# A head-normalised attention kernel: q and k prepared apart at the start, the order planned on exact times, the last stores behind the branch

## The chip, the cores and the metric

The kernel runs on one core of a Trainium2 chip. The metric is the device time of one execution in microseconds (us). Before the change it is 594.08 us, the median of three runs (593.81 to 594.42). A core has five engines that work at the same time and meet through semaphores: TensorE (PE, matrix products; its weight loads are shown as PEld), VectorE (DVE), ScalarE (ACT), GpSimd (POOL) and SyncE (SP), which mostly issues DMA transfers. Each engine takes its instructions strictly in the order of its own queue.

## The reference

There are 32 heads of 2048 rows with 20 elements each, in bf16. Rows of q and k are divided by their length, so logits are cosines times a factor t per head; then softmax and the product with v:

```python
qn = q / (jnp.sqrt((q * q).sum(axis=-1, keepdims=True)) + eps)
kn = k / (jnp.sqrt((k * k).sum(axis=-1, keepdims=True)) + eps)
logits = jnp.einsum('bhqd,bhkd->bhqk', qn, kn) * t[None, :, None, None]
attn = _softmax(logits, axis=-1)
return jnp.einsum('bhqk,bhkd->bhqd', attn, v)
```

## The kernel before, in words

**Tiles.** Four heads form a group; there are eight groups, and in each four blocks of 512 q columns. Group and block together are a "superblock" (32 in all). In a superblock each head has 16 "units": 128 rows of k against 512 columns of q. A unit's logits come from one matmul (`qk_mm`, seen at L793) into PSUM, its exponentials are taken, and they are multiplied with v by one or more matmuls (`pv_mm`, L815) that accumulate in one PSUM bank per superblock. There are 32*64 = 2048 units. A column of ones beside v gives the softmax's sum.

**Two ways to take an exponential.** Most units go in "waves" of two to ACT (L995), through `psA` into `pA`. The others are taken by DVE: one instruction "P1" (L361) turns logits in `psD` into the bits of a 16-bit float in `dI`, and two shifted copies `dS` (mostly on POOL, L374) correct it; such a unit needs four matmuls with v where an ACT unit needs one. One of the four uses `vhalf`, half of v. This way is used only if t is not too large. So the program has a branch: DVE takes the largest t into `tmx` (L578, the "flag"), each engine loads it at its own place in its queue (L1432) and branches (L1433) into the plan with both ways or the one with ACT alone.

**Preparation.** q and k are loaded with 16 rows per partition; rows 0 to 3 of the first group come first. DVE squares (L291), sums (L294); ACT takes the square root (L309); DVE adds eps (L310), takes the reciprocal (L322), multiplies q's by t (L344) and scales k and q into `kpad` and `qpad` (L338). In the first group rows 0 to 3 are turned by matmuls with an identity (L624) and copied to `kT` and `qT` (L636 on ACT, L639 on DVE); rows 4 to 7 of k likewise a little later (L658, L664); rows 8 to 15 of k and 4 to 15 of q by a DMA transpose issued by SP (L446). Later groups go through DMA transposes wholly and are prepared while the group before is computed. Before the first turning PE multiplies zeros, 18 matmuls of 512 columns (L616, `HEAT0`), and small ones (L612) later where it would stand idle. The identity itself is built on DVE out of counters (L559 to L568).

**The order.** Nothing is scheduled on the chip. When the program is built, `make_plan` simulates all engines on a clock of 0.005 us steps with cost constants (`dve`, `ACT0`, `TS`, `LOAD0` and others), decides at each step what each engine takes next by readiness and priorities, and writes each engine's instructions down in that order; semaphore waits follow from the dependencies. DVE's way starts when the share of issued units in the first group passes `D_FROM`. `ORDER` is a string: for every ten waves one character picks a variation of the rules from `CHOICES`. In this simulation an instruction begins on a step of the clock, after the engine is free.

**The end.** After the last matmul DVE transposes the sums out of PSUM (L386), takes reciprocals (L400) and multiplies (L401); two stores, one issued by SP and one by ACT (L458), write the last part. SP first waits for all older stores (L1416). Both stores are the last instructions inside the branch; then SP waits for the two (L1439), and all engines meet at the end of the function (L173).

Of the kernel before, what the change touches and what calls it, by code (L numbers as in the profile page):

```python
# [33 lines left out]
ORDER = "01i6e8h7238em08g57h5hi2i0gi1j2i0lgea8aa50a567i6538abh965h237050"  # L34

PARTS = ((0, 4), (4, 16))
NH = 4
# [7 lines left out]
D_FROM = 0.12  # L45
# [14 lines left out]
DT = 0.005  # L60
END_MIN = 1
TS = .213
PACK = 0
JOINT = -9
HEAT0 = 18
# [6 lines left out]
ACT0 = .0633  # L72
# [84 lines left out]
def bass_standalone__qk_norm__prompt_kernel(  # L157
# [15 lines left out]
    with ExitStack() as es:  # L173
# [45 lines left out]
        out_sems = {}  # L219

# [27 lines left out]
        def prep_ops(hg, r0, r1, a0=0, a1=2, pool=False):  # L248
# [106 lines left out]
            return ops  # L355

# [112 lines left out]
        def make_plan(share):  # L469
# [42 lines left out]

            def want_dve(op, prio):
# [44 lines left out]
            for ap_, x, key in zs:  # L558
                want_dve(Op("DVE", "z", lambda e, ap_=ap_, x=x: e.memset(ap_, x), ["idn"] * (key[0] == "idb"), [key], 0.07, 0.3), 0)  # L559
            n0 = [("num", a) for a in range(8)]  # L560
            for b in (1, 2, 3):
                want_dve(Op("DVE", "z", lambda e, b=b: e.tensor_single_scalar(n4[:, :, b:b + 1], n4[:, :, 0:1], float(b), ALU.add),
                            n0, [("num", -b)], 0.08, 0.4), 0)
            nums = n0 + [("num", -b) for b in (1, 2, 3)]
            want_dve(Op("DVE", "z", lambda e: e.transpose(numT, num), nums, ["numT"], 0.15, 0.4), 0)
            want_dve(Op("DVE", "z", lambda e: e.tensor_tensor(numE, num, numT, ALU.is_equal), nums + ["numT"], ["numE"], 0.15, 0.4), 1.6)
            i4, e4 = idn[:, :].rearrange("p (a b) -> p a b", b=32), bass.AP(accT, numE.offset, [numE.ap[0], [0, 4], [1, 32]])
            want_dve(Op("DVE", "z", lambda e: e.tensor_tensor(i4, i4, e4, ALU.mult), ["idn", "numE"] + [("idb", a) for a in range(4)], ["idn", ("accT", 0)], 0.25, 0.4), 1.6)  # L568
# [6 lines left out]
            def t_load():  # L575
# [4 lines left out]
                want_dve(dve("z", H, R1, lambda e: e.tensor_copy(tb2[:, :, 0, :], tb16[:, :].rearrange("p (g h) -> p g h", h=NH)), ["tb1", "tb"], ["tb2"]), 1.45)  # L580
# [13 lines left out]
            for o in prep_ops(0, 0, 4, 0, 2):  # L594
                if o.name == "nrm":
                    o.eng = "ACT"
                    act_ops.append(P.link(o))
                    a = Op("ACT", "tab", lambda e: e.activation(act_scr[:, 16:32], act_scr[:, 16:32], ACT.Exp),
# [23 lines left out]
            psQ = psD[:, QW:2 * QW]  # L622
            for w_, pad, T, bank, key in (("k", kpad, kT, psD, ("psD", 0)), ("q", qpad, qT, psO, ("psD", OB(0)))):
                mms = [lambda e, r=r, w_=w_, pad=pad, bank=bank: e.matmul((bank if w_ == "k" or r < 2 else psQ)[:, r * 128:(r + 1) * 128],  # L624
                                                                   pad[0][:, r, :, :].rearrange("p h d -> p (h d)"), idn[:, :])
                       for r in range(4)]
                op = Op("PE", "T" + w_, None, [(w_ + "pad", 0, r) for r in range(4)] + [(w_ + "z", 0), "idn"],
                        [key] + [("psD", 1)] * (w_ == "q"))
                op.info = mms
                pe_pre.append(P.link(op))  # L630

            kk, qq = [("kT", 0, r) for r in range(4)], [("qT", 0, r) for r in range(4)]
# [16 lines left out]
            pe_mid = []  # L649
            gate = ("qT", 0, 1)  # L650
            for r0, r1, a0, a1 in ((4, 16, 1, 2), (4, 16, 0, 1)):
                for o in prep_ops(0, r0, r1, a0, a1):
                    if o.name == "sq":
                        o.reads.append(gate)
# [833 lines left out]
```

## Time and profile before

| what | value |
|---|---|
| median of three runs | 594.08 us |
| the profiled execution's own time | 594.49 us |
| its span, first to last instruction | 592.7 us |
| ACT busy / DVE busy / PE busy / POOL busy | 580.4 / 574.6 / 581.3 / 500.9 us |
| first exp begins | 9.47 us |
| first P1 begins | 23.32 us |
| last store issued | 588.52 us |
| waves on ACT, units on DVE | 628, 792 |

A line of instructions in order of time has the start, the stretch it covers, engine, line, operation, output and inputs, the count merged into it, and in brackets the engine's idle time before with what ended it. A line of groups has the busy time and the mean duration of one instruction in ns; since instructions overlap in an engine's pipeline, a mean duration is longer than the distance from one to the next. The lines of one source line's queue instructions (a letter q behind the engine) give the count, the duration in ns as least, median and most, and the first and last start. Landing is the time from a transfer's issue until its data are there.

### The profile page before, as it was taken

The numbers are of one execution on the slowest core, as the hardware profiler recorded it, in microseconds if no ns is written. First come the engines' busy times: TensorE is split into PE (matmuls) and PEld (weight loads), VectorE is DVE, ScalarE is ACT, GpSimd is POOL, SyncE is SP. The second block draws the span as 40 slices with busy tenths as digits, with TensorE's granted clock in tenths as the row PEclk, the third lists the DMA queues.
The fourth block names the chain that finished last, engine by engine and source line by source line (L and its number), as shares of the span: only waits on it lengthen the run. The fifth ranks groups of instructions, "written<-read, shape, count | busy, mean of one in ns | idle before, by whom it ended". The sixth has DMA issues, their size and how long they took to land.

```text
span 592.7 us, 16383 instructions
## 1 busy us (share of the span) xinstructions
PE 581.3 (98%) x6768; PEld 160.2 (27%) x6768; DVE 574.6 (97%) x1016; ACT 580.4 (98%) x636; POOL 500.9 (84%) x951
## 2 busy tenths in 40 slices
PE   8999999999999999999999999999999999999996
PEld 4432222322223222232223222222222232222221
DVE  7999999999999999999999999999999999999993
ACT  6999999999999999999999999999999999999995
POOL 2488899878988799887998889987999978999994
PEclk9999999999999999999999999999999999999999
DMA  8700405205051131504033005330406104010000
GB/s 116 108 2 14 104 2 45 47 8 110 3 59 32 31 86 13 79 1 101 19 22 71 1 19 100 24 69 10 92 2 76 32 2 72 2 25 4 7 11 11
DMA packets 132145, 24.20 MB, mean 41 GB/s; under 512 B 121312, under 2 KB 132064, under 8 KB 132064
## 3 DMA queue, kind: packets, MB, share of 16 engines
q1 hardware_dynamic: 131264, 22.96, 24.6%
q8 instruction: 55, 0.90, 0.6%
q14 instruction: 26, 0.21, 0.1%
q10 hardware_dynamic: 800, 0.12, 0.1%
HBM read 7.87 MB, written 2.62 MB: 18 GB/s over the span
## 4 chain that ended last, share of the span: by engine, by line
ACT 87%; PE 10%; DVE 2%; POOL 1%; issue 0%
ACT pA L995 87%; PE psD L815 4%; PE psA L793 3%; PE psA L616 1%; PE psD L612 1%; POOL dS L374 1%; DVE dI L361 0%; PE psD L793 0%; PE psD L749 0%; DVE ssum L294 0%; DVE accT L386 0%; DVE sqs L291 0%; DVE kpad L338 0%; PE psD L616 0%; DVE ost L401 0%
## 5 line engine op out<-in xcount | busy, mean ns | idle before, releaser
L995 ACT ACTIVATE pA<-psA 128x1024 f16<-128x1024 f32 (+1 forms) x628 | 576.2, 1201 | 0.5 <-PE psD L793 0.2
L374 POOL INT64_ADD dS<-dI x935 | 494.5, 545 | 71.3 <-DVE ost L401 14.3
L361 DVE TENSOR_SCALAR dI<-psD 128x512 int16<-128x512 f32 (+1 forms) x768 | 488.1, 695 | 4.3 <-PE psD L793 2.5
L793 PE MATMUL psA<-qT,kT 32*128 32x512 bf16 x1256 | 246.4, 384 | 3.7 <-ACT pA L995 1.0
L793 PE MATMUL psD<-qT,kT 32*128 32x512 bf16 x795 | 237.6, 383 | 0.1
L815 PE MATMUL psD<-dS,vaug 128*22 128x512 f16 x1584 | 201.2, 383 | 0.1
L815 PE MATMUL psD<-pA,vaug 128*22 128x512 f16 (+1 forms) x1256 | 181.1, 383 | 0.3 <-POOL dS L374 0.3
L815 PE MATMUL psD<-dI,vaug 128*22 128x512 f16 x792 | 133.9, 383 | 0.0
L815 PE MATMUL psD<-dI,vhalf 128*22 128x512 f16 x792 | 131.4, 383 | 0.0
L793 PEld LDWEIGHTS psA<-qT,kT 32*128 32x128 bf16 x1256 | 59.0, 90 | 241.1 <-ACT pA L995 235.5
L793 PEld LDWEIGHTS psD<-qT,kT 32*128 32x128 bf16 x795 | 57.3, 91 | 11.1 <-DVE dI L361 4.8
L815 PEld LDWEIGHTS psD<-dS,vaug 128*22 128x22 bf16 x1584 | 42.9, 89 | 58.2 <-issue 38.2
L815 PEld LDWEIGHTS psD<-pA,vaug 128*22 128x22 bf16 x1256 | 39.6, 89 | 49.6 <-issue 41.2
L815 PEld LDWEIGHTS psD<-dI,vhalf 128*22 128x22 bf16 x792 | 29.7, 89 | 27.4 <-issue 20.0
L815 PEld LDWEIGHTS psD<-dI,vaug 128*22 128x22 bf16 x792 | 30.3, 89 | 23.4 <-issue 16.7
L386 DVE STREAM_TRANSPOSE accT<-psD 128x512 f32<-128x512 f32 x32 | 22.6, 705 | 4.6 <-PE psD L815 4.6
L401 DVE TENSOR_TENSOR ost<-accT,rec 128x320 bf16<-128x320 f32 x32 | 17.0, 532 | 0.1
L264 DVE TENSOR_TENSOR sqs<-qk 128x1280 bf16<-128x1280 bf16 x14 | 11.7, 835 | 0.0
L749 PE MATMUL psD<-ind,sqT 128*128 128x128 bf16 x140 | 11.3, 220 | 0.0
L612 PE MATMUL psD<-zt 128*128 128x128 bf16 x123 | 10.3, 221 | 0.0
L749 PEld LDWEIGHTS psD<-ind,sqT 128*128 128x128 bf16 x140 | 7.9, 98 | 4.5 <-issue 3.6
L612 PEld LDWEIGHTS psD<-zt 128*128 128x128 bf16 x123 | 7.0, 98 | 4.9 <-issue 4.9
(59 smaller groups left out, 84.7 us busy)
## 6 DMA issues: line engine op xcount, KB each, us to landing
vaug<-in_v_dram SPq DMA_DIRECT2D x32, 80.0 KB, 4.3
qk<-in_k_dram SPq DMA_DIRECT2D x7, 320.0 KB, 4.0
out_dram<-ost SPq DMA_DIRECT2D x28, 80.0 KB, 1.9
qk<-in_q_dram SPq DMA_DIRECT2D x6, 320.0 KB, 4.3
qk<-in_q_dram SPq DMA_DIRECT2D x4, 80.0 KB, 3.0
out_dram<-ost SPq DMA_DIRECT2D x7, 40.0 KB, 2.1
qk<-in_k_dram SPq DMA_DIRECT2D x1, 240.0 KB, 3.7
qk<-in_q_dram SPq DMA_DIRECT2D x1, 240.0 KB, 4.3
```

What stands on the lines that cost most here:

```text
L264: ops.append(dve("sq", w_, R2, lambda e, o=sq, x=x3: e.tensor_tensor(o, x, x, ALU.mult), [("qk", b, a, i) for i in parts] + [("qkx", b, i) ...
L361: lambda e: e.tensor_scalar(dst, psD[:, pb * QW:(pb + n) * QW], 1024.0 * LOG2E, 15360.0 - 1024.0 * LOG2K + SHIFTS[0], ALU.mult, ALU.add),
L374: lambda e: e.int64_add(o.bitcast(U64), x.bitcast(U64), add), rd, wr)
L386: return dve("drain", QW, R1, lambda e: e.transpose(accT[:, 16 * b:16 * b + 16, :].rearrange("p b d -> p (b d)"), psO_(sb)), [("psD", OB(s ...
L401: dve("omul", 320 * n, R1, lambda e: e.tensor_tensor(dst, num, rcb, ALU.mult), at + ar, [("ost", hg % 2, g) for g in range(g0, g1)]),
L612: return lambda e: e.matmul(bank, zt[:, 0:128], zt[:, 0:n], start=False, stop=False, skip_group_check=True)
L616: o.info = [lambda e: e.matmul(psO[:, :], zt[:, 0:128], zt[:, :])] + [(lambda e, i=i: e.matmul(psA[:, (i % 3) * QW:(i % 3 + 1) * QW], zt[: ...
L749: mms = [lambda e, g=g, j=j: e.matmul(dst, sqT[:, (5 * g + j) * 128:(5 * g + j + 1) * 128], ind[:, j, 96 - 32 * g:224 - 32 * g], start=g + ...
L793: return lambda e: e.matmul(dst, lhsT, rhs, tile_position=(32 * hh, 0))
L815: return lambda e: e.matmul(dst, lhsT, rhs, start=first, stop=last, skip_group_check=True, tile_position=(0, 32 * hh))
L995: a = Op("ACT", "exp", lambda e, s=src, d=dst: e.activation(d, s, ACT.Exp), [("psA", slot)], [("pA", pslot, i) for i in range(WAVES[slot]) ...
```

## The change

The diff has four parts.

1. Rows 0 to 3 of the first group are prepared by a new function `first_ops`: q and k each have their own square, sum, square root, eps and reciprocal, written down with q ahead; k's scaling is cut into rows 0 and 1, and rows 2 and 3. The turnings follow: q first, then k's rows 0 and 1, then k's rows 2 and 3 into another bank, with 3, 3 and 6 small zero products around them (`WARM`). The copies are q's by DVE and ACT, k's first two rows by ACT, its next two by DVE. `HEAT0` goes from 18 to 11. The identity's last steps get the first priority. The later preparation of q no longer waits for rows 4 to 7 of `kT`.
2. DVE's way of taking exponentials starts earlier (`D_FROM` from 0.12 to 0.07).
3. The simulation lets an ACT or DVE instruction begin at the exact time within a step at which engine and inputs are free (`exact`); a DVE instruction costs 0.065 instead of 0.069 beside its elements, ACT's constant is 0.0634 instead of 0.0633, and there is a new `ORDER`.
4. The last two stores stand behind the branch and wait for a semaphore of their own (`fin_sem`), which the last multiplication sets. SP's waits for the older stores also move behind the branch.

```diff
-ORDER = "01i6e8h7238em08g57h5hi2i0gi1j2i0lgea8aa50a567i6538abh965h237050"
+ORDER = "42711eji12k7d5l79657bj0ldifi7fc7g9jcbm72glei3ma9gglljgm190dig74"
-D_FROM = 0.12
+D_FROM = 0.07
-HEAT0 = 18
+HEAT0 = 11
+WARM = (3, 3, 6)
+CPQ = ("DVE", "ACT")
-ACT0 = .0633
+ACT0 = .0634
...
-            o = Op("DVE", name, emit, reads, writes, cost=0.069 + c + ncols_fix,
+            o = Op("DVE", name, emit, reads, writes, cost=0.065 + c + ncols_fix,
...
+        def first_ops():
+            sqf, redf, nrmf, epsf, invf, scf = [], [], [], [], [], []
+            T_ = lambda tl, a: tl[:, a, :, 0:4]
+            for a, pad, nm in ((0, qpad, "qpad"), (1, kpad, "kpad")):
...
+                for c0, c1 in ((0, 4),) if a == 0 else ((0, 2), (2, 4)):
...
+            n_sq[0] = 0
+            return sqf + redf + nrmf + [epsf[0]] + invf[0:2] + [scf[0], epsf[1], invf[2]] + scf[1:]
...
+            def exact(eng, op, other=0.0):
+                st = max(free_[eng], ready_at(op) or 0.0, other)
+                return st if now - DT < st <= now else now
...
-            for o in prep_ops(0, 0, 4, 0, 2):
+            for o in first_ops():
...
+            pe_pre.extend([warm(WARM[0]), turn("q", 0, 4, [psO, psO, psQ, psQ], [("psD", OB(0)), ("psD", 1)]), warm(WARM[1]),
+                           turn("k", 0, 2, [psD] * 2, [("psD", 0)]), warm(WARM[2])])
+            pe_mid = [turn("k", 2, 4, [psK] * 2, [("psD", 2)])]
...
-            copy("ACT", kT, psD, 0, 128, [("psD", 0)], kk[:1])
-            copy("DVE", qT, psO, 0, 256, [("psD", OB(0))], qq[:2])
-            copy("ACT", qT, psQ, 256, 512, [("psD", 1)], qq[2:])
-            copy("ACT", kT, psD, 128, 512, [("psD", 0)], kk[1:])
+            copy(CPQ[0], qT, psO, 0, 256, [("psD", OB(0))], qq[:2])
+            copy(CPQ[1], qT, psQ, 256, 512, [("psD", 1)], qq[2:])
+            copy("ACT", kT, psD, 0, 256, [("psD", 0)], kk[:2])
+            copy("DVE", kT, psK, 256, 512, [("psD", 2)], kk[2:])
...
-                finish(a, now, a.cost, a.lat)
-                free_["ACT"] = now + a.cost
+                st = exact("ACT", a)
+                finish(a, st, a.cost, a.lat)
+                free_["ACT"] = st + a.cost
...
+                st = exact("DVE", o, lock[0] if o.port else 0.0)
+                finish(o, st, o.cost, o.lat)
+                free_["DVE"] = st + o.cost
...
+                if o.name == "out" and o.sem in ends:
+                    assert o is P.order[e][-1] and [d.sem for d in o.deps] == [fin_sem]
+                    continue
...
+            if e == "SP":
+                for x in plans[0][0].order["SP"]:
+                    if x.name == "out" and x.sem not in ends:
+                        eng.wait_ge(x.sem, 16)
+            for o in plans[0][0].order[e][-1:]:
+                if o.name == "out":
+                    eng.wait_ge(fin_sem, 1)
+                    o.emit(eng).then_inc(o.sem, 16)
```

More of the change, by code (lines that the diff above doesn't have):

```diff
@@ L219, in bass_standalone__qk_norm__prompt_kernel @@
         out_sems = {}
+        fin_sem = sem("s_fin")
         def dma_sem():
@@ L910, in step_heat @@
                 nonlocal pe_mode, pe_t
-                if in_use() >= S.HEAT or cur == NSB or not cur_free():
+                if not waves or in_use() >= S.HEAT or cur == NSB or not cur_free():
                     return False
@@ L1220, in step_dve @@
                             return True
-                finish(o, now, o.cost, o.lat)
-                free_["DVE"] = now + o.cost
+                st = exact("DVE", o, lock[0] if o.port else 0.0)
+                finish(o, st, o.cost, o.lat)
+                free_["DVE"] = st + o.cost
                 return True
@@ L1410, in issue @@
             P, waits = plan
-            outs = [o for o in P.order["SP"] + P.order["ACT"] if o.name == "out"]
             for o in P.order[e][i0:i1]:
-                if e == "SP" and o.name == "out" and o.sem is ends[0]:
-                    for x in outs:
-                        if x.sem not in ends:
-                            eng.wait_ge(x.sem, 16)
+                if o.name == "out" and o.sem in ends:
+                    assert o is P.order[e][-1] and [d.sem for d in o.deps] == [fin_sem]
+                    continue
                 for s_, val in waits[id(o)]:
```

78 lines of the change are left out of this document (49 added, 29 removed).

## The prediction, made before the changed kernel ran

> **What bounds the kernel now.** I read the page's busy times and groups first, then the instructions in order of time at both ends, then the chain.
>
> ```profile
> PE 581.3 (98%) x6768; PEld 160.2 (27%) x6768; DVE 574.6 (97%) x1016; ACT 580.4 (98%) x636; POOL 500.9 (84%) x951
> ...
> L995 ACT ACTIVATE pA<-psA 128x1024 f16<-128x1024 f32 (+1 forms) x628 | 576.2, 1201 | 0.5 <-PE psD L793 0.2
> L361 DVE TENSOR_SCALAR dI<-psD 128x512 int16<-128x512 f32 (+1 forms) x768 | 488.1, 695 | 4.3 <-PE psD L793 2.5
> ```
> ```profile
> 51.27 517.24 ACT pA L995 x564
> ```
>
> Two engines share the exponentials. ACT takes 628 waves of two units (1256), DVE the other 792 of 2048 units (768 instructions, 24 of them double). The chain's middle is 564 exps in 517.24 us: 0.917 each. An instruction's own duration includes its pipeline, so a pitch is a stretch less one duration (1.20 for an exp by its group, 0.68 for a single P1 by shape), over the count less one:
>
> ```profile
> 195.23 19.35 ACT L995 ACTIVATE pA<-psA 128x1024 f16<-128x1024 f32 x21
> ```
> ```profile
> L361 DVE TENSOR_SCALAR dI<-psD 128x512 int16<-128x512 f32 x744 | 460.8, 679 | 3.2 <-PE psD L793 1.4
> ```
> ```profile
> 361.09 7.80 DVE L361 TENSOR_SCALAR dI<-psD 128x512 int16<-128x512 f32 x13
> ```
> ```profile
> 361.09 3.01 DVE L361 TENSOR_SCALAR dI<-psD 128x512 int16<-128x512 f32 x5
> ```
> ```profile
> 561.14 11.65 DVE L361 TENSOR_SCALAR dI<-psD 128x512 int16<-128x512 f32 x19
> ```
>
> A good stretch of exps has (19.35-1.20)/20 = 0.907. In a good stretch of P1, eight more add 7.80-3.01 = 4.79, or 0.599; an ordinary one gives (11.65-0.68)/18 = 0.609. So neither engine has a long idle time, and both wait a little for PE's written-out order. Time can come from the start, the end, the split of units, and those small waits.
>
> **The start.** DVE, ACT and PE up to the first exp:
>
> ```profile
> 1.65 6.38 PE L616 MATMUL psA<-zt 128*128 128x512 bf16 x17
> ...
> 3.68 0.49 DVE L291 TENSOR_TENSOR sqs<-qk 128x640 bf16<-128x640 bf16 x1 [0.62 <-DMA qk<-in_q_dram]
> ...
> 4.09 0.28 DVE L568 TENSOR_TENSOR idn<-idn,accT 128x128 bf16<-128x128 bf16 x1
> ...
> 4.29 0.81 DVE L294 TENSOR_REDUCE ssum<-sqs 128x32 f32<-128x640 bf16 x1
> ...
> 5.02 0.18 DVE L578 TENSOR_REDUCE tmx<-tb 128x1 f32<-128x32 bf16 x1
> ...
> 5.14 0.23 ACT L309 ACTIVATE nr<-ssum 128x32 f32<-128x32 f32 x1 [2.29 <-DVE ssum L294]
> 5.39 1.28 ACT L598 ACT_TABLE_LOAD   x1
> 5.40 0.18 DVE L310 TENSOR_SCALAR rsa<-nr 128x32 f32<-128x32 f32 x1
> ...
> 5.62 0.35 DVE L322 RECIPROCAL rn<-rsa 128x32 f32<-128x32 f32 x1
> ...
> 6.34 0.15 PEld L616 LDWEIGHTS psA<-zt 128*128 128x128 bf16 x1 [0.28 <-issue]
> 6.41 0.17 DVE L344 TENSOR_TENSOR rn<-rn,tb 128x16 f32<-128x16 f32 x1
> 6.61 0.49 DVE L338 TENSOR_TENSOR qpad<-qk,rn 128x320 bf16<-128x320 bf16 x1
> ...
> 6.77 0.76 PEld L616 LDWEIGHTS psA<-zt 128*128 128x128 bf16 x4 [0.28 <-issue]
> ...
> 8.51 0.42 DVE L639 CAST qT<-psD 128x256 bf16<-128x256 f32 x1 [1.41 <-PE psD L624]
> 8.79 0.48 ACT L636 ACTIVATE kT<-psD 128x384 bf16<-128x384 f32 x1
> 8.97 0.73 DVE L291 TENSOR_TENSOR sqs<-qk 128x640 bf16<-128x640 bf16 x2
> ...
> 9.47 4.69 ACT L995 ACTIVATE pA<-psA 128x1024 bf16<-128x1024 f32 x5 [0.19 <-PE psA L793]
> ```
>
> q is ready at 7.10 (6.61+0.49), but PE works off zeros until 8.03: they come every 0.43 up to 6.77, then every 0.21. So the zeros set the start. Eleven of them end at 1.65+10*0.43 = 5.95, and q's path takes over. On DVE an independent successor starts 0.08 before an end (3.68+0.49 to 4.09), a dependent one about 0.03 after. The identity's product (0.20 of pitch between square and sum) moves ahead of 3.68, into the 0.62 of waiting for q. Squares and sums of 320 elements, from the groups by shape:
>
> ```profile
> L294 DVE TENSOR_REDUCE ssum<-sqs 128x16 f32<-128x320 bf16 x2 | 1.0, 486 | 0.1
> ...
> L291 DVE TENSOR_TENSOR sqs<-qk 128x320 bf16<-128x320 bf16 x2 | 0.6, 318 | 0.0
> ```
>
> By these: squares 3.68 and 3.92, sums 4.16 and 4.57, the flag 4.98, eps of q 5.08 (its square root has run since 4.69), reciprocal 5.29 to 5.54, times t 5.58 to 5.75, then q's scaling 5.84 (after k's reciprocal) to 6.33. That is 0.77 earlier, though DVE has five instructions more (two squares, sums, eps and reciprocals for one, and k's scaling in two).
>
> PE's branch waits for the flag:
>
> ```profile
> L1432 PEldq TENSOR_LOAD <-tmx x1: 483/483/483, 5.2 to 5.2; - x1
> ```
> ```profile
> L1433 PEldq COMPARE_BRANCH  x2: 89/1801/3513, 6.1 to 586.0; - x2
> ```
>
> From the flag's load to the branch's end it is 0.95, under zeros now. With the flag at its old place it ends at 6.2 again, after the eleven zeros, so three small zeros end near 6.5, and the turning of q ends at 7.0 to 7.1. ACT has two square roots (0.23 each), then the table load (1.28), ready by 6.9, under cover of DVE; without that cover it would add directly. The copies of q run 7.15 to 7.57 on DVE and ACT; k's two rows are turned meanwhile, and their copy (0.38) ends near 7.9. From a last copy's end (8.93) to the first exp (9.47) it took 0.53. First exp: 8.45, **1.0 less**. Bounds: 0.3 less (PE slow throughout and every join late) to 1.3 less.
>
> One row speaks against it: PE's pitch halves only at 6.77, after 5.5 us without a gap, and now it pauses between 5.95 and 6.2. Slow to the first exp, turnings and first products cost 0.45 more, and the total is 0.45 higher. [...]
>
> **The units that DVE takes.** DVE's own start:
>
> ```profile
> 14.69 0.69 DVE L664 CAST kT<-psD 128x512 bf16<-128x512 f32 x1 [0.49 <-PE psD L658]
> ...
> 23.32 1.23 DVE L361 TENSOR_SCALAR dI<-psD 128x1024 int16<-128x1024 f32 x1 [1.10 <-PE psD L793]
> ```
>
> DVE's later preparation begins at 7.5 instead of 8.97 (1.47); q's part no longer waits for kT (0.49); with D_FROM 0.07 instead of 0.12, P1s begin at 18 issued units instead of 31, near 8.45+7*0.917 = 14.9 (the ninth wave is issued when the seventh exp is done) instead of 23.32, so the 1.10 of idleness goes; one copy more costs 0.34. The halved v, of lower priority than all this, now comes after the first P1s; their results wait for it in a ring of 28 slots, some 17 us of P1. POOL, idle until then, starts its additions earlier. Together 2.7 us, or 4.4 units at 0.609. ACT's 1.0 is 2.2 units. Over 2/0.917+1/0.609 = 3.82 units per us, 6.6 units are 1.7 us for start and split together.
>
> Behind that a wait becomes late. Rows 8 to 15 of kT come by DMA, and SP issues them behind loads that no compute holds up:
>
> ```profile
> 11.79 5.33 SPq L437 DMA_DIRECT2D vaug<-in_v_dram  x3
> 17.16 2.05 SPq L446 DMA_TRANSPOSE kT<-kpad  x1
> ```
> ```profile
> kT<-kpad SPq DMA_TRANSPOSE x1, 4.0
> ```
>
> They land at 21.2. Rows 0 to 7 are 32 units: today issued by about 23, then by about 18.8 (18 units at 14.9, then 3.6 per us). The planner books 1.4 per v load where three took 5.33, so it does not see this. PE then stands with everything behind it; ACT, with two waves in hand, idles some 1.4 (3.1 units), while DVE partly has preparation left. I take 6.6-3.1 = 3.5 units, **0.9 less** for start and split (ends: 1.7 less, and 1.9 more in the second rival).
>
> **The end.** Queue instructions of the function's closing line, and the last stores:
>
> ```profile
> 587.94 0.49 DVE L401 TENSOR_TENSOR ost<-accT,rec 128x320 bf16<-128x320 f32 x1
> 588.46 0.67 ACTq L458 DMA_DIRECT2D out_dram<-ost  x1
> ```
> ```profile
> L173 SPq DRAIN  x1: 13/13/13, 591.1 to 591.1; - x1
> L173 ACTq DRAIN  x1: 81/81/81, 592.4 to 592.4; - x1
> ```
>
> The span ends at 592.7, on ACT's drain. ACT leaves the branch only after issuing its store (589.13) and arrives 3.3 later; SP, which saw both stores land, drains at 591.1. With the stores behind the branch, ACT jumps after dispatching its last exp (584.8, the row below) and, 3.3 later (PE's own jump took 3.5, above), arrives near 588.1 to 588.3, before the product is done at 588.43: the jump lies under drain, reciprocal and product. SP's drain is then last, **1.3 less**. Bounds: 0.4 less (ACT a microsecond late, its store late too) to 1.4. SP's sixteen waits for older stores move behind the jump too, and are over long before the last product. The last exp's start:
>
> ```profile
> L995 ACT ACTIVATE pA<-psA x628: 1018/1196/1347, 9.5 to 584.8; 128x1024 f16<-128x1024 f32 x156, 128x1024 bf16<-128x1024 f32 x1
> ```
>
> **The order in between.** New constants and the ORDER string rewrite all queues. The planner no longer rounds each ACT and DVE start up to 0.005, and a DVE step costs 0.004 less: P1 0.598, as in the undisturbed stretch. The trace cannot show the new order. Best end: all exps and P1s at their undisturbed pitch, 628*0.010 = 6.3 and 792*0.010 = 7.9 less on the two, so about 7 together. Worst: DVE is given units that it cannot hold, 3 to 5 more. The chip's mean pitches lie within 2% of the undisturbed ones and PE waits remain, so I stay near zero: **0.9 less**.
>
> **Sum.** 0.9+1.3+0.9 = 3.1 of the profiled span: 592.7 to 589.6. That execution took 594.49, 0.41 above the median; from the median, 594.08-3.1 = 591.0.
>
> **Rivals.** (1) Slower: DVE becomes the bound. It is 97% busy, and from 23.3 to 582.3 hardly idle. Each P1 unit beyond 792 costs 0.609, against 2.7+1.3 gained: even at 799 units, and ten more give +2.1, 596.2. For it: the planner's DVE got cheaper by 1%, which invites more units; against it: the pitch it now assumes is the undisturbed one. 0.09. (2) The kT rows fall behind all four v loads, landing near 23 (5.33/3 = 1.8 later): ACT idles 2.9, which takes the start's 1.0 and 1.9 more; with the end's 1.3 and no gain in the middle, 594.7. For it: q's preparation now fills k's gaps on DVE, delaying kpad; against it: loads do not depend on it. 0.12. (3) The new order removes half of the small waits: 3 less, 588.0. 0.20. (4) The start does not move, PE being slow or the branch late: 591.9. Inside the forecast, which has 0.59 with it.
>
> Shares: faster (below 592.9) 0.79, same 0.12, slower 0.09; 0.2%, 1.2 us, is what a measurement can tell from nothing. The range runs from 587.6, past rival 3, to 594.3, most of the way to rival 2; rival 1 is left out.
>
> **What would show it.** First exp at 8.4 to 8.5; q's scaling done at 6.3; PE's pitch still 0.43 for all big zeros; first P1 near 15; PE and ACT idle between 18.8 and 21.2 with kT's DMA as releaser; ACT's drain no later than SP's; P1 units between 792 and 799 and exps between 624 and 628. Wrong it goes if P1 units pass 799, if ACT's mean pitch rises over 0.92, or if DVE waits for PE in the middle.

## The result, and the profile after

The changed kernel takes 599.69 us (median of four runs, 599.26 to 599.96), the kernel before beside it 593.94 (593.57 to 594.42). The ratio is 1.0096, with a 95% interval of 1.0078 to 1.0113: it became 1% slower. The prediction said 591.0 with a range up to 594.3, so it is wrong in sign and size. The profiled execution took 599.8 us, its span is 598.1 in place of 592.7. Three executions of the experiments below ran at a clearly lower granted clock than most others of their kernel (769.92 us at 0.602 with the new start alone, 599.38 and 599.63 us at 0.977 and 0.976 with one addition of POOL ahead); they count in the medians and not in the ratios.

The page of the kernel after: busy times, the clock that PE was granted in 40 slices of 15 us, and the two groups of exponentials.

```profile
PE 583.2 (98%) x6744; PEld 156.6 (26%) x6744; DVE 575.8 (96%) x1034; ACT 577.6 (97%) x632; POOL 505.0 (84%) x947
...
PEclk9759999999999999999999999999999999999999
...
L1037 ACT ACTIVATE pA<-psA 128x1024 f16<-128x1024 f32 (+1 forms) x624 | 573.6, 1212 | 11.9 <-PE psA L833 7.7
...
L393 DVE TENSOR_SCALAR dI<-psD 128x512 int16<-128x512 f32 (+1 forms) x781 | 492.7, 689 | 14.5 <-PE psD L833 12.1
```

ACT has four exps fewer (624 for 628), DVE eight units more (800 for 792). Against that ACT was idle for 11.9 us before its exps, where it was 0.5 before, and the clock is below full in the second and third slice. Everything unusual lies ahead of 50 us.

The account is easiest on ACT. The most frequent distance between the starts of two exps is 0.9035 us in both traces, so a span is the first exp's start, plus (exps - 1) times 0.9035, plus what the single distances exceed 0.9035 by in sum ("waits"), plus what follows the last exp's start ("tail"):

| | first exp | exps | waits | of these before 50 us | tail | span |
|---|---|---|---|---|---|---|
| before | 9.47 | 628 | 8.8 | 0.9 | 8.0 | 592.7 |
| after | 7.77 | 624 | 21.1 | 13.1 | 6.3 | 598.1 |
| difference in time, from unrounded values | -1.7 | -3.6 | +12.3 | +12.3 | -1.7 | +5.3 |

So three terms went the right way, by 7.0 us together, more than the 3.1 that were predicted. One term, the waits of the first 50 us, took 12.3. Beyond 50 us the waits are the same in both. ACT's exps of that stretch, in order of time:

```profile
7.77 3.77 ACT L1037 ACTIVATE pA<-psA 128x1024 bf16<-128x1024 f32 x4 [0.49 <-PE psA L833]
12.56 8.36 ACT L1037 ACTIVATE pA<-psA 128x1024 f16<-128x1024 f32 x9 [1.02 <-PE psA L833]
26.14 1.02 ACT L1037 ACTIVATE pA<-psA 128x1024 f16<-128x1024 f32 x1 [5.22 <-PE psA L833]
27.86 1.02 ACT L1037 ACTIVATE pA<-psA 128x1024 f16<-128x1024 f32 x1 [0.70 <-PE psD L833]
29.36 1.02 ACT L1037 ACTIVATE pA<-psA 128x1024 f16<-128x1024 f32 x1 [0.48 <-PE psD L833]
```

There are three places: 1.0 of idleness ahead of 12.56, 5.2 ahead of 26.14, and then an exp every 1.5 us up to 41.5. The first two come from waits of PE, in whose queue the next products for ACT stand behind these:

```profile
11.80 0.40 PE L855 MATMUL psD<-pA,vaug 128*22 128x512 bf16 x4 [0.93 <-DMA vaug<-in_v_dram]
...
19.22 0.39 PE L833 MATMUL psA<-qT,kT 32*128 32x512 bf16 x2
24.51 0.60 PE L855 MATMUL psD<-dS,vaug 128*22 128x512 f16 x2 [4.90 <-POOL dS L406]
```

At 19.6 PE reaches the first product with a shifted copy `dS`, which POOL has not made. DVE's part was ready early, its first three P1s start at 16.84, and POOL did nothing that the profile shows (DVE, POOL, and POOL's queue instructions at the line of the additions):

```profile
16.84 2.56 DVE L393 TENSOR_SCALAR dI<-psD 128x1024 int16<-128x1024 f32 x3
```
```profile
17.64 0.39 POOL L571 MEMSET vaug<- 128x64 bf16 x1
23.77 2.37 POOL L406 INT64_ADD dS<-dI  x4 [5.73 <-issue]
```
```profile
L406 POOLq MODIFY_POOL_CONFIG  x2: 11/11/11, 18.0 to 18.0; - x2
```

A configuration instruction ran at 18.0, and the first addition at 23.77, 5.7 us later; "issue" says that the engine waited for nothing that the profile shows. The kernel before has the same thing, at the same place in POOL's queue:

```profile
L374 POOLq MODIFY_POOL_CONFIG  x2: 11/11/11, 19.2 to 19.2; - x2
```
```profile
25.35 7.38 POOL L374 INT64_ADD dS<-dI  x14 [6.93 <-DVE dI L361]
```

There the addition followed 6.2 us after the configuration, and the idle time was put down to DVE's P1. With the first P1 at 23.32 hardly anything waited for it. So both traces have a delay of about 6 us (5.7 and 6.2) between the configuration and POOL's first addition, without an instruction in it; what fills it they do not show.

The third place is the clock. Windows of the kernel after: PE's, PEld's, DVE's, ACT's and POOL's busy time with counts, granted clock, share of DMA, GB/s:

```profile
20.00:25.00 5.00, 0.49 (x4) 0.13 (x4) 0.56 (x1) 0.92 (x2) 1.24 (x3) 0.69 1.07 202
25.00:30.00 5.00, 5.00 (x35) 1.02 (x31) 2.58 (x4) 2.68 (x3) 2.68 (x6) 0.50 0.22 41
30.00:40.00 10.00, 10.00 (x69) 2.54 (x66) 6.18 (x11) 6.71 (x8) 6.08 (x12) 0.50 0.01 2
40.00:50.00 10.00, 10.00 (x117) 2.87 (x115) 9.09 (x19) 9.27 (x11) 7.17 (x14) 0.88 0.01 3
```

During the idle time the granted clock fell to half, at 21.9, and it stayed there until 42.4, although PE was busy without a gap from 24.5 on. At half the clock PE is the bound, and both other engines wait for it.

The end of the kernel after, DVE, ACT's and SP's stores, and the drains of the function's end:

```profile
594.74 0.49 DVE L433 TENSOR_TENSOR ost<-accT,rec 128x320 bf16<-128x320 f32 x1
```
```profile
595.26 0.67 ACTq L490 DMA_DIRECT2D out_dram<-ost  x1
```
```profile
L175 ACTq DRAIN  x1: 582/582/582, 596.0 to 596.0; - x1
...
L175 SPq DRAIN  x1: 13/13/13, 597.8 to 597.8; - x1
```

ACT now drains right behind its store and SP comes last, as predicted; it was ACT, 3.3 us behind its store.

### The profile page after: what moved, and what is told of

The parts are those of the page before. It is cut to its first block, busy times and chain, and to the rows that moved or that the text cites. A ratio compares the mean times of both kernels' runs of the same rounds, so it can differ in the third digit from the quotient of the medians.

```text
span 598.1 us, 16346 instructions
## 1 busy us (share of the span) xinstructions
PE 583.2 (98%) x6744; PEld 156.6 (26%) x6744; DVE 575.8 (96%) x1034; ACT 577.6 (97%) x632; POOL 505.0 (84%) x947
## 4 chain that ended last, share of the span: by engine, by line
ACT 90%; PE 7%; SPq 1%; DMA 1%; issue 1%; DVE 1%; POOL 0%
ACT pA L1037 90%; PE psD L855 3%; PE psA L833 2%; SPq L469 1%; DMA vaug<-in_v_dram 1%; PE psD L651 1%; PE psD L789 0%; PE psD L833 0%; SPq L459 0%; DVE sqs L267 0%; DVE accT L418 0%; DVE dI L393 0%; POOL dS L406 0%; DVE ost L433 0%; SPq L613 0%
## 5 line engine op out<-in xcount | busy, mean ns | idle before, releaser
L1037 ACT ACTIVATE pA<-psA 128x1024 f16<-128x1024 f32 (+1 forms) x624 | 573.6, 1212 | 11.9 <-PE psA L833 7.7
L833 PE MATMUL psD<-qT,kT 32*128 32x512 bf16 x801 | 244.4, 388 | 0.0
L855 PE MATMUL psD<-dS,vaug 128*22 128x512 f16 x1600 | 203.5, 385 | 4.9 <-POOL dS L406 4.9
L855 PE MATMUL psD<-pA,vaug 128*22 128x512 f16 (+1 forms) x1248 | 178.6, 386 | 0.9 <-DMA vaug<-in_v_dram 0.9
L855 PE MATMUL psD<-dI,vaug 128*22 128x512 f16 x800 | 136.8, 385 | 0.0
L855 PEld LDWEIGHTS psD<-pA,vaug 128*22 128x22 bf16 x1248 | 38.4, 89 | 47.1 <-issue 42.4
L789 PE MATMUL psD<-ind,sqT 128*128 128x128 bf16 x140 | 12.8, 233 | 0.0
L267 DVE TENSOR_TENSOR sqs<-qk 128x1280 bf16<-128x1280 bf16 x14 | 11.8, 843 | 0.0
L432 DVE RECIPROCAL rec<-accT 128x16 f32<-128x16 f32 x32 | 7.5, 234 | 0.1
L325 DVE RECIPROCAL rn<-rsa 128x128 f32<-128x128 f32 (+1 forms) x9 | 7.4, 827 | 0.0
```

The costliest lines, as they stand in the source:

```text
L267: ops.append(dve("sq", w_, R2, lambda e, o=sq, x=x3: e.tensor_tensor(o, x, x, ALU.mult), [("qk", b, a, i) for i in parts] + [("qkx", b, i) ...
L325: add("inv", lambda e: e.reciprocal(rn_, ra), [K("ra")], RN[a0:a1], R1, n * 5 * R1)
L432: dve("rec", 16 * n, R1, lambda e: e.reciprocal(rc, aT[:, :, D]), at, ar, 16 * n * 5 * R1),
L789: mms = [lambda e, g=g, j=j: e.matmul(dst, sqT[:, (5 * g + j) * 128:(5 * g + j + 1) * 128], ind[:, j, 96 - 32 * g:224 - 32 * g], start=g + ...
L833: return lambda e: e.matmul(dst, lhsT, rhs, tile_position=(32 * hh, 0))
L855: return lambda e: e.matmul(dst, lhsT, rhs, start=first, stop=last, skip_group_check=True, tile_position=(0, 32 * hh))
```

## The experiments

Two theories stood against each other. A: the 12.3 us are POOL's invisible 5.7 us, and the clock that PE's idleness costs behind it. (The expectations call this delay the loading of the additions' code. That is the author's reading; no trace shows it.) B: the new order itself is at fault (DVE has too many units, or the parts of the change don't fit each other), and the gap would open elsewhere. All times are medians, each with its ratio to the kernel before on the same chip; readings of a trace are those of one profiled execution.

### The gap filled with zeros, so that the clock stays

The wait for POOL stays, but PE multiplies 80 zeros of 128x128 ahead of it:

```diff
+                if e == "PE" and any(s_ is sems["POOL"] and val >= first_add.get(id(P), 1e9) for s_, val in waits[id(o)]):
+                    first_add.pop(id(P))
+                    for _ in range(FILL):
+                        eng.matmul(psO[:, 0:128], zt[:, 0:128], zt[:, 0:128], start=False, stop=False, skip_group_check=True)
                 for s_, val in waits[id(o)]:
                     eng.wait_ge(s_, val)
```

> The changed kernel with 80 small zero products put into PE's queue just ahead of its first wait for a shifted copy, where it stood idle from 19.6 to 24.4; all queues are otherwise the same. If the half clock is caused by PE's idleness and costs what follows it: the wait of ACT near 20 to 26 us remains (5 us), the clock stays at full and exps from 27 us on come every 0.92 instead of 1.5: about 6 us less, 593.5. If the half clock comes from something else, the time stays at 599 to 600.

593.13 us, ratio 0.999 (0.9972 to 1.0008); nine of ten executions took 593.0 to 593.5, and one 598.12 at a granted clock of 0.988. The windows of this run have the full clock throughout:

```profile
20.00:30.00 10.00, 9.31 (x134) 5.86 (x130) 4.45 (x9) 5.00 (x7) 4.98 (x11) 1.00 0.83 123
30.00:50.00 20.00, 19.91 (x244) 5.79 (x240) 19.87 (x37) 20.00 (x24) 17.14 (x33) 1.00 0.01 2
```

The waits between 25 and 50 us fall from 6.5 to 0.25, and the long one near 20 stays (5.2 over the usual distance, 5.4 in the kernel after). So the lost clock alone is worth 6.3 us, and the gap the other 5.4. Zeros do nothing for the kernel but keep the clock.

### The same zeros behind the gap

The same loop with `FILL = 48` stands behind the wait for POOL: the clock falls, and PE then gets products over the full 128 rows and columns.

> The changed kernel with 48 small zero products on the whole array put just behind PE's first wait for a shifted copy (near 24.4), where the clock is already halved and PE then works without a break for 18 us at half speed. If the clock returns when the whole array works, not when PE is merely never idle (its products use 32 of 128 rows or 22 of 128 columns each), full clock is back by about 28 to 32 instead of 42.4, the exps' 1.5 us distance ends there, and the time lies 0 to 4 us under the changed kernel's. If being busy is enough, the clock would have come back by itself, and these zeros (5 us at half speed) only cost: 2 to 5 us more.

598.39 us (two executions), ratio 1.0064 (1.0046 to 1.0082). Windows:

```profile
24.00:30.00 6.00, 5.01 (x48) 5.04 (x48) 0.00 (x0) 0.00 (x0) 2.37 (x4) 0.50 0.50 94
30.00:31.00 1.00, 1.00 (x10) 0.27 (x7) 0.00 (x0) 0.00 (x0) 0.00 (x0) 0.65 0.07 16
31.00:32.00 1.00, 1.00 (x11) 0.30 (x9) 0.35 (x1) 0.56 (x1) 0.00 (x0) 1.00 0.00 0
```

The half clock lasts from 23.9 to 30.7, where it took 20.5 us without these zeros. So here products over the whole array brought the clock back sooner, and a busy PE alone did not: in the kernel after, PE was busy all the time from 24.5 to 37.3, almost only with products of 32 rows (with `kT`) and of 22 columns (with v), at half the clock, and the clock came back behind the 128x128 products of the next group's sums, at 37.3 to 40.9. Such products are no condition, though: with `D_FROM` alone (below) the clock came back at 33.7 without any since 24.3.

### One addition of POOL ahead of the others

Only POOL's queue is written anew, all other orders stay: the two selections without their wait for DVE, then one addition on a scratch tile (`prm`), and the zeros of the second group's tiles later. So POOL's first addition, with the delay ahead of it, comes before POOL's results are due (this is the run with POOL's code first of the expectations).

```diff
+            prime = Op("POOL", "prime", lambda e: e.int64_add(prm[:, :].bitcast(U64), prm[:, :].bitcast(U64), 0))
+            prime.deps = [se[1], next(o for o in po if "prm" in o.writes)]
+            for o in se:
+                o.deps = [d for d in o.deps if d.eng == "POOL"]
...
+            P.order["POOL"] = po[:i0] + se + [prime] + rest[:k] + zs + rest[k:]
```

> The changed kernel's own orders on PE, ACT, DVE and SP; on POOL alone the two selections come first, then one 64-bit addition on a scratch tile, and the zeros of the second buffers come after 30 us of the planner's time. The addition's code should then be there by about 18. Theory A: PE does not wait for POOL at 19.6, the half clock goes, and of the 12 us of exps' waits before 50 us at most 2 or 3 remain (kT's rows 8 to 15 land at 21.5, which PE needs near 20): a span of 587 to 589, a time of 589 to 591. If something other than POOL's code holds PE there (the landing alone), ACT still idles 4 us or more near 20 and the time stays over 593.

591.27 us, ratio 0.9968 (0.994 to 0.9995; the two medians alone would give 0.9946). POOL and ACT in the profiled execution (589.86 us, span 588.1):

```profile
11.84 0.76 POOL L578 TENSOR_SCALAR_AFFINE_SELECT ind<-ind 128x160 bf16<-128x160 bf16 x2 [7.17 <-issue]
19.03 0.39 POOL L1378 INT64_ADD prm<-prm  x1 [6.43 <-DVE dI L395]
19.41 3.19 POOL L408 INT64_ADD dS<-dI  x4
```
```profile
12.67 9.62 ACT L1040 ACTIVATE pA<-psA 128x1024 f16<-128x1024 f32 x10 [0.54 <-PE psA L836]
22.93 16.62 ACT L1040 ACTIVATE pA<-psA 128x1024 f16<-128x1024 f32 x18 [0.64 <-PE psD L836]
```

The delay is still 6.2 us (the configuration is now at 12.8), but it ends at 19.0. The 5.2 us of ACT's idleness are gone, the clock is full (1.00 from 20 to 50 us), and the waits come to 10.5 us. With the same orders on the four other engines, 8.4 us of the median are back: theory A holds, B falls. In five of the twelve executions the clock still fell (595.5 to 599.6 us; their mean granted clock is 0.976 to 0.989, so it stood at half for some 13 to 29 us); the other seven took 589.65 to 591.56.

### Zeros ahead of two smaller gaps, and of one of them

What is left at the start are PE's first wait for v (0.45 us in the run above) and that for the second transpose of k (0.55). First 10 zeros ahead of each, on top of the addition ahead:

```diff
+                if e == "PE" and o.start < 30.0 and any(s_.name.startswith("s_dma") for s_, val in waits[id(o)]):
...
+                    for _ in range(FILL):
+                        eng.matmul(psO[:, 0:128], zt[:, 0:128], zt[:, 0:128], start=False, stop=False, skip_group_check=True)
```

> The kernel after, POOL's queue ordered so that its code is loaded before the first additions (as in the run that gave 591.27 us), and 10 zero products of 128x128 ahead of PE's first wait for v's rows and 10 ahead of its first wait for the second transpose of k (idle 0.45 and 0.55 us there). Theory: what is left of the spread of that run (589.65 to 599.63 us, granted clock 0.976 to 0.989 in the long ones) is the clock falling in a stretch with such gaps; with them filled most times lie at 589.5 to 591.0 us and the median at or under 590.8. Rival: the clock falls for another gap (PE's 1.5 us behind the branch, or later ones); then the spread and the median stay, 591.3 and times up to 599. Either way the zeros can cost up to 0.5 us where a transfer is early.

592.01 us, ratio 0.9964 (0.995 to 0.9978): over the 590.8 that was expected, with five of six times at 591.2 to 592.2 and one of 597.78. That one is the profiled execution, so its trace can be read. PE's wait for k's transpose, and the windows behind it:

```profile
22.44 0.39 PE L837 MATMUL psD<-qT,kT 32*128 32x512 bf16 x2 [1.20 <-DMA kT<-kpad]
```
```profile
25.00:30.00 5.00, 5.00 (x34) 0.79 (x34) 3.30 (x6) 3.27 (x4) 3.01 (x7) 0.50 0.40 78
30.00:35.00 5.00, 5.00 (x40) 2.01 (x32) 2.64 (x5) 2.88 (x3) 2.95 (x6) 0.50 0.00 0
```

Here the transpose was issued 0.5 us later than in the run with the addition ahead (18.1 for 17.6), PE was idle for 1.2 us, and the half clock lasts from 23.4 to 37. That the idleness is its cause is argued from this one execution. Then 28 zeros (1.6 us) at this place alone, and none ahead of v (against the run just told):

```diff
-FILL = 10
+FILL = 28
...
-                if e == "PE" and o.start < 30.0 and any(s_.name.startswith("s_dma") for s_, val in waits[id(o)]):
+                if e == "PE" and o.start < 30.0 and any(s_.name == "s_dma9" for s_, val in waits[id(o)]):
```

> The kernel after with POOL's code loaded first, without zeros ahead of the wait for v's rows, and with 28 zero products (1.6 us) in place of 10 ahead of PE's first wait for the second transpose of k. In the profiled run with 10 and 10 zeros, k's transpose left SP 0.5 us later (18.1 in place of 17.6), PE was idle 1.20 us behind its zeros, and the clock stood at half from then to 37 us. Theory: this gap decides whether the clock falls; with 1.6 us of zeros it is covered wherever the transpose lands between 21.6 and 22.5, so all times lie at 590 to 592 us, none over 594, and where it lands early the zeros cost up to 0.4 us. Rival: the clock falls for something else (PE's own wait for v's rows, 0.5 to 1.4 us near 11 us, or the phase of the clock's first opening); then times of 595 to 600 us come again.

590.76 us (590.40 to 591.45), ratio 0.9943 (0.9929 to 0.9956). No long time came in five runs, as this theory has it; five executions are few against a drop that comes in some only (in one of six before), so this part is not settled. The rows of PE and ACT:

```profile
21.74 1.74 PE L1479 MATMUL psD<-zt 128*128 128x128 bf16 x28
23.41 0.39 PE L837 MATMUL psD<-qT,kT 32*128 32x512 bf16 x2
```
```profile
24.64 16.62 ACT L1041 ACTIVATE pA<-psA 128x1024 f16<-128x1024 f32 x18 [1.77 <-PE psD L837]
```

Here the zeros ended 1.1 us after the transpose had landed (22.41), more than the 0.4 that was expected, and ACT was idle for 1.8 us; the median is still the best of all, 0.6% faster than the kernel before and 1.5% (8.9 us) than the change as it was made.

### Two other ways to mend it

In the first the selections and one addition on scratch were given to the planner, with 6 us booked for the delay, so that it orders everything anew:

```diff
+            o = Op("POOL", "prime", lambda e: e.int64_add(prm[:, :].bitcast(U64), prm[:, :].bitcast(U64), 0), ["ind", "prm"], ["prm"], PRIME, PRIME + 0.1)
+            o.alone = True
+            want_dve(o, 1)
```

> The changed kernel with POOL's queue rearranged: the two selections of the indicator no longer wait for kpad, one small 64-bit addition on a scratch tile follows them (booked at 6.0 in the planner), and the zeros of the second buffers come later. D_FROM stays 0.07. Theory A: the code is loaded by about 18, additions follow the first P1s at once, PE has no idle time over 1 us and the clock stays up after the start: 585 to 588. Rival B: no gain over 3 us.

600.38 us, ratio 1.0106 (1.009 to 1.0123): no gain, as rival B had it. The start is mended, the first 25 us have 1.8 us of waits, but the new plan is worse in all else: 630 exps in place of 624 (+5.4), a tail of 9.3 in place of 6.3, and a new hole in the second group,

```profile
88.71 12.02 ACT L1044 ACTIVATE pA<-psA 128x1024 f16<-128x1024 f32 x13 [2.03 <-PE psD L840]
```

`ORDER` stayed what it was, and a change to what is planned draws another plan.

In the second, on top of the addition ahead, SP issues the transposes of k and q ahead of the next four v loads:

```diff
+            t2 = [next(o for o in so if o.name == x) for x in ("Tk", "Tq")]
+            v1 = [o for o in so if o.name == "ldv"][4:8]
...
+            P.order["SP"] = so[:i0] + t2 + v1 + mid + so[i1:]
```

> As the run with POOL's code first, and SP issues the DMA transposes of kT (rows 8 to 15) and qT ahead of the four loads of the next group's v. If the landing of kT is the next wait (the prediction's second rival), kT lands near 18 instead of 21.5 and the time falls by another 0.5 to 2 us, to 587.5 to 590. If it is not, no difference to that run within 0.3.

593.9 us, ratio 1.0006 (0.9981 to 1.0032): 2.6 more than without it, which neither side expected; two of twelve executions took 599.5 and 601.1. The wait for k is gone from PE, and two others are there:

```profile
12.80 0.40 PE L858 MATMUL psD<-pA,vaug 128*22 128x512 bf16 x4 [1.85 <-DMA vaug<-in_v_dram]
...
31.48 0.44 PE L792 MATMUL psD<-ind,sqT 128*128 128x128 bf16 x5 [1.88 <-DMA sqT<-sqs]
```

The second is a price of the move: SP now stands idle until k's and q's rows are ready, the v loads end at 24.0 in place of 17.6, and the transposes of the squares behind them begin at 24.05 in place of 21.04. The first, the group's own v, was not moved; in this execution its loads took 0.8 us longer to issue (5.97 for 5.21). The clock fell behind each (0.51 in the mean from 15 to 18 us, 0.52 from 32 to 35).

### The parts of the change alone

The changed kernel with DVE's way starting as late as before:

```diff
-D_FROM = 0.07
+D_FROM = 0.12
```

> The changed kernel with D_FROM set back to 0.12. Theory A (POOL loads the code of its 64-bit additions only from 18.0 us on and has it 5.7 us later; with P1s from 16.8 PE reaches the first product with a shifted copy before that, stands from 19.6 to 24.4, and the clock falls to half until 42.4): P1s start after 21 us, the additions are ready in time, no idle time of PE over 1 us, no half clock after the start, and 11 to 13 us less than the changed kernel: about 587.5. Rival B (the new order and its 8 more P1 units are too much for DVE): about 597 to 600, with a mean exp pitch over 0.925 beyond 50 us.

596.71 us, ratio 1.0047 (1.0031 to 1.0064). The gap and the half clock are gone without any zeros (mean granted clock 1.0): ACT runs through from 12.40,

```profile
12.40 48.71 ACT L1037 ACTIVATE pA<-psA 128x1024 f16<-128x1024 f32 x53 [0.83 <-PE psA L833]
```

and the waits are 9.6 us in all. But this plan has 632 exps and 784 units, eight exps (7.2 us) more than after: the 587.5 that was expected had left this out. The time lies near rival B's, but B's sign, a mean pitch over 0.925 beyond 50 us, is not there (0.917, as in the kernel before).

The kernel before with DVE's way starting early:

```diff
-D_FROM = 0.12
+D_FROM = 0.07
```

> The kernel before with D_FROM 0.07 and nothing else. Theory A: P1s start near 16, POOL's additions not before 24 to 25.5, PE waits several us for them, the clock falls to half, and the kernel is slower by 6 to 13 us: 600 to 607. Rival C (the loss needs the other parts too, the order or the earlier first exp): within 2 us of 594.

609.07 us, ratio 1.0248 (1.0231 to 1.0265), over the 600 to 607 that were expected. Waits of 19.3 us are 10.5 more than before, with the half clock from 20.0 to 33.7; four more exps add 3.6, and the tail 1.0. PE waits for k's transpose, as the prediction had it for the kernel after, and then for POOL:

```profile
21.41 0.61 PE L793 MATMUL psA<-qT,kT 32*128 32x512 bf16 x2 [2.30 <-DMA kT<-kpad]
24.34 0.60 PE L815 MATMUL psD<-dS,vaug 128*22 128x512 f16 x2 [2.32 <-POOL dS L374]
```

So the early start of DVE's way is what uncovers POOL's delay, in either kernel. The clock came back here without a product over the whole array: from 24.3 to 33.7 PE's records are products of 32 rows or 22 columns alone. Windows, in the columns given above:

```profile
26.82:30.23 3.41, 3.41 (x22) 0.49 (x16) 2.90 (x4) 2.76 (x3) 2.98 (x7) 0.50 0.00 0
30.23:33.65 3.42, 3.42 (x29) 0.56 (x25) 2.39 (x4) 2.24 (x3) 2.13 (x4) 0.50 0.00 0
33.65:37.06 3.41, 3.41 (x37) 1.15 (x35) 2.43 (x8) 3.19 (x4) 2.08 (x5) 1.00 0.02 7
```

The kernel before with the last stores behind the branch:

```diff
+                if o.name == "out" and o.sem in ends:
...
+                    continue
...
+            for o in plans[0][0].order[e][-1:]:
+                if o.name == "out":
+                    eng.wait_ge(fin_sem, 1)
+                    o.emit(eng).then_inc(o.sem, 16)
```

> The kernel before with only the last two stores and SP's older waits moved behind the branch. The prediction's step: ACT's drain, last today at 592.4, comes before SP's, and the end is 1.3 us earlier (bounds 0.4 to 1.4), so 592.7 where the kernel before has 594.0. If the jump is not what ends the kernel: no change within 0.3.

592.87 us, ratio 0.9971 (0.9961 to 0.9981). The tail goes from 8.0 to 6.5, and the drains stand as in the kernel after:

```profile
L173 ACTq DRAIN  x1: 583/583/583, 589.0 to 589.0; - x1
...
L173 SPq DRAIN  x1: 13/13/13, 590.8 to 590.8; - x1
```

This part is a gain of its own (1.6 us by the medians, 1.5 by the tail), whatever the start does.

The kernel before with the new start alone (`first_ops`, `HEAT0 = 11`, the turnings and copies as in the diff of the change):

```diff
-HEAT0 = 18
+HEAT0 = 11
...
-            for o in prep_ops(0, 0, 4, 0, 2):
+            for o in first_ops():
```

> The kernel before with the start of the kernel after (first rows of q and k apart, 11 zeros), all else as before. It plans 780 half-waves for DVE in place of 792, so 634 exponentials on ACT in place of 628. Theory of the sum (first exponential + exponentials x 0.9035 + waits + tail): first exponential at 7.8 to 8.4 us, -1.1 to -1.7; six more exponentials, +5.4; waits as before or up to 1 us more: 597.5 to 599 us. Rival, as the prediction summed it: the start is worth its own 1.0 to 1.3 us and the shares of the engines hardly move: 592.5 to 593.5 us.

606.19 us, ratio 1.0188 (1.0169 to 1.0207), far above both expectations; the four times are 605.26, 605.39, 606.98 (the profiled one) and 769.92. The first exp does come at 7.80, and six more exps cost the 5.4 that were counted. What was not counted is 4.0 more of waits, mostly at the start, beginning with PE's wait for v (1.39 us; the clock falls behind it, and the products with `kT` take 0.61 from 15.12 on in place of 0.39), and a tail longer by 4.7: the last exp starts at 592.5, but PE is some 5 us behind with the products with v, and DVE waits for the last of them:

```profile
598.24 0.81 PE L850 MATMUL psD<-pA,vaug 128*22 128x512 f16 x10
```
```profile
599.11 0.72 DVE L417 STREAM_TRANSPOSE accT<-psD 128x512 f32<-128x512 f32 x1 [7.67 <-PE psD L850]
```

The kernel before with the new `ORDER`, the simulation without rounded beginnings and its two new constants:

```diff
-ORDER = "01i6e8h7238em08g57h5hi2i0gi1j2i0lgea8aa50a567i6538abh965h237050"
+ORDER = "42711eji12k7d5l79657bj0ldifi7fc7g9jcbm72glei3ma9gglljgm190dig74"
...
+            def exact(eng, op, other=0.0):
+                st = max(free_[eng], ready_at(op) or 0.0, other)
+                return st if now - DT < st <= now else now
```

> The kernel before with the new ORDER string and the simulation without rounded beginnings, DVE's share still from D_FROM .12. It plans 796 half-waves for DVE in place of 792, so 626 exponentials in place of 628. Theory of the sum: -1.8 for two exponentials, waits beyond 50 us as before (mean pitch 0.917), start and tail as before: 591.5 to 593 us. Rival of the prediction: the simulation now says when things happen, and the small waits between exponentials (8.8 us in all) are halved: 588 to 590 us.

601.6 us, ratio 1.0125 (1.0109 to 1.014), another miss of both. Two exps fewer, but waits of 13.4 us, some of them in the middle,

```profile
399.91 1.94 ACT L999 ACTIVATE pA<-psA 128x1024 f16<-128x1024 f32 x2 [0.79 <-PE psD L797]
402.93 18.82 ACT L999 ACTIVATE pA<-psA 128x1024 f16<-128x1024 f32 x20 [1.07 <-PE psD L797]
```

and a tail longer by 4.1; the first exp came 0.4 later. So start, `D_FROM` and `ORDER` have no price of their own. Each change of one draws another plan, with its own number of exps and its own backlog at the end, and that weighs up to 10 us; only the last part can be added to another kernel and keep its value.

## Why the prediction was wrong

**The start** was predicted at 1.0 less with 1.3 as the bound, and measured 1.7: first exp at 7.77. In the sum q's path took over from 5.95 and the first exp came 2.5 later; q's scaling began at 5.63 in place of 5.84, and the granted clock was full already at 4.85, so turnings and first products went at the fast pitch. The clock was full before PE's pause (5.56 to 6.03), so the slow start that was weighed there did not come. How early the clock opened differed between executions of nearly the same start: at 4.85 here, and at 3.9 in the run with one addition of POOL ahead, whose ten zeros from 1.67 on took 3.44 us in place of 3.90. The first exp of the kernel after and its variants lies between 7.77 and 8.36; the two do not go together, since the run that opened at 3.9 has its first exp at 8.36. But 1.2 of the 1.7 were given back at once: PE reaches its first product with v before v has landed (11.8), which the sum did not look at.

**The end** was predicted at 1.3 less, at most 1.4, and measured 1.7, alone 1.5. Its mechanism held: the jump of the engines at the end of the branch lies under other work, and SP's drain is last. The other 0.2 is that the last multiplication began 3.0 after the last exp's start and not 3.2.

**The units** were predicted as 792 to 799 on DVE, and are 800, with 624 exps, one unit past the prediction's own sign of going wrong. Four exps fewer are 3.6 us. The first P1 came at 16.84, not near 15. DVE could hold them: in the run with one addition of POOL ahead its last P1 starts at 580.8, and in the kernel before at 581.6. So the first rival is not what happened, though the result came out on its side. The mean pitch of all exps, 0.937, also passed the prediction's mark of 0.92, but by the first 50 us alone; beyond them it is 0.917.

**The order in between** was put at 0.9 less; the waits beyond 50 us are equal in both kernels, so the third rival, with half of them gone, is not seen. What the change gained here lies in the split between ACT and DVE, which no part of it gives alone (796 units with the order, 784 with `D_FROM`, 780 with the start), and not in smaller waits.

**The rows of `kT`** were to land at 21.2 and hold up PE and ACT by 1.4. They landed at 21.7, not near 23 as in the second rival (whose 2.9 of idleness would be 1.4 + 1.8 = 3.2 by the prediction's own terms), and with POOL out of the way PE waits 0.55 us for them, not the 2.4 from 18.8 to 21.2, and ACT 0.64. The mechanism was right, and the size less than half. In the kernel after nothing of it is seen, since PE stood before POOL until 24.5.

**The step that failed** is one clause of "The units that DVE takes": "POOL, idle until then, starts its additions earlier." It could hardly: the first P1 came 6.5 us earlier (16.84 for 23.32), the first addition 1.6 (23.77 for 25.35). POOL's first addition follows its configuration by about 6 us (5.7 here, 6.2 before), and POOL's queue reaches the configuration only at 18.0, behind selections and zeros that wait for DVE; the first product with a shifted copy stands at 19.6. Early P1s took away the cover, 5.4 us of waits came of it, and the idle PE lost its clock for 20.5 us, which cost 6.5 more; with the 1.2 for v that is nearly all of the 13.1 us of waits before 50 us. The trace of before puts POOL's idle time down to DVE's P1, and the prediction took that as it stood; the P1 had ended at 24.55 (23.32+1.23), 0.8 us before POOL began, and the configuration stood 6.2 us ahead. With that delay moved ahead (591.27) and the clock kept (590.76) the kernel runs at what was predicted, 591.0; that it agrees so well is partly chance, since the terms were larger on either side.

## What to carry to other kernels

When a change makes an engine's first work of a kind due earlier, look for what that first work carries: an instruction of configuration in the queue followed by several us of "issue", or by a wait whose releaser had long been done, may be a delay that can be moved to where the engine is idle: here 5.7 us, and with it moved the 5.2 us of ACT's idleness were gone. Price a gap of PE not by its length but by the clock behind it: here 5 us of idleness cost 6.5 more, and full-size zero products in the gap bought those back without removing the wait. And parts of a change that share a planned order can't be priced, nor tested, one at a time.

## What the runs showed of the hardware

- In these runs a busy PE did not always bring the clock back. In the kernel after the clock stood at half for 20.5 us (21.9 to 42.4), and PE was 100% busy from 24.5 on; with 48 products of 128x128 put there it came back within 5.7 us of their first one (24.99 to 30.7). In the kernel before with `D_FROM` 0.07 it came back behind 9.3 us of products of 32 rows or 22 columns (24.34 to 33.65). What decides when it comes back, these runs do not show.
- The length of PE's idle time did not decide alone whether the clock fell. It fell at 20.0, 0.9 us into an idle time of 2.30 us that began at 19.11, in the kernel before with `D_FROM` 0.07, and within 1 us after an idle time of 1.20 us (22.44) with 10 zeros ahead of two gaps; it stayed after 1.51 us, ahead of 6.62, with one addition of POOL ahead, where the products around were 128x128.
- POOL's additions began 5.5 to 6.2 us after their configuration where nothing else held them (18.0 to 23.77 in the kernel after, 19.2 to 25.35 in the kernel before), and the selections came behind 6.8 to 7.9 us without an instruction of POOL (4.3 to 11.3 in the kernel after). Both were of the same size where the additions' delay was moved ahead: 6.2 and 7.2 us with one addition ahead, 5.9 and 7.9 with the 28 zeros as well. What POOL does in these times, no trace shows.
